# A sliding-window attention and GELU MLP stack on one core: a new written-out order of all engine queues

## The chip, the cores and the metric

The kernel runs on one NeuronCore of one Trainium2 chip. The metric is the time of one execution in device microseconds (us), less being better. A core has five engines that work through queues of their own, strictly in order, and that meet only at semaphores: PE (TensorE, matrix products), ACT (ScalarE, activation functions), DVE (VectorE), POOL (GpSimd) and SP (SyncE, which here only issues DMAs). PE writes its products into PSUM, which has eight banks of 512 float32 values per partition; ACT and DVE read them from there.

## What is computed

Two rounds of the same two layers over `x` of 2048 tokens by 512 channels in bf16. The attention has 32 heads of 16 channels and a causal window of 256 keys; the MLP is 512 to 1792 to 512 with a tanh GELU. The weights are the same in both rounds.

```python
def _A_ref(x, wqkv, wo):
    H = 32; Dh = D // H; W = 256
    q, k, v = (x @ wqkv) split into heads
    scores = einsum("bhqd,bhkd->bhqk", q, k) * (Dh ** -0.5)
    mask = (idx[:, None] - idx[None, :] >= 0) & (idx[:, None] - idx[None, :] < W)
    p = softmax(where(mask, scores, -1e9))
    o = einsum("bhqk,bhkd->bhqd", p, v)
    return o merged @ wo

def _B_ref(x, w1, b1, w2, b2):
    return gelu(x @ w1 + b1) @ w2 + b2

x = A_x
x = x + _A_ref(_layernorm(x), A_wqkv, A_wo)
x = x + _B_ref(_layernorm(x), B_w1, B_b1, B_w2, B_b2)
x = x + _A_ref(_layernorm(x), A_wqkv, A_wo)
x = x + _B_ref(_layernorm(x), B_w1, B_b1, B_w2, B_b2)
```

## The kernel before

**Tiles.** The 2048 tokens are 16 tiles of 128 rows, kept in SBUF as `X`. The two rounds make 32 tile passes, handled as 16 blocks of two tiles (block 0 to 7 are round one, 8 to 15 round two) for the attention, and as ten MLP jobs of two or four tiles (`JOBS`).

**The steps of a block.** For the layer norm DVE runs `bn_stats` (L588) and `bn_aggr` (L590), the inverse standard deviation is an add (`vp`, L594, POOL or DVE) and a power (`pw`, L600, POOL), and DVE writes the normalised tile `xn` (L610). A DMA transposes it (L615), except for the first four and the last two of the 64 normalised tiles, which PE transposes (`tp`, L622). Then PE makes Q and K (groups `q` and `k`, two each per block) and V (group `v`, one per tile); these, the output projection `op`, the first MLP product `m` (14 groups per job) and the second `y` (one per tile, 14 steps) are the *dense products*. All of them go through `pe_group` (L636): a group takes one PSUM bank at its first step, and its steps stand in the queue as nodes of their own (`m0_3.0`, `m0_3.1` and so on), so steps of other groups, or scores, can stand between them. The bank comes free when the group's result has been read out: K by DVE (`ke`, L670, 1.2 us), Q and V by DVE (L577) or ACT (L579), `op` and `y` by DVE (L832, L874), the first six `m` groups by DVE (L854) with a GELU on ACT afterwards (L857), the other eight by ACT (L862).

**Attention.** A block has ten *visits* (the first block of each round has five). A visit is one PE node `sc` (L737) that fills four banks with 2048 columns of scores, two ACT exponentials `ex` (L744), each of which reads two banks and frees them, and one to three masks `mk` (L765, DVE or POOL) that zero what lies outside the window in the exponentials. Twice per block a PE node `pv` (L787, 128 small matmuls, 64 in the first block of a round) multiplies the exponentials with V into two banks; DVE transposes those (`od`, L796), takes the reciprocal of the softmax sums (`rc`, L800), DVE or POOL normalises (`nm`, L804), and DVE transposes back (`ot`, L810) for the output projection.

**The order.** Nothing about the order is decided while the kernel is built. `_Plan.add` records 3080 nodes with their dependencies. Three written-out lists do the rest. `_ORDER` (L167) is one sequence of all nodes; each engine's queue is the nodes of that engine in that sequence. `_ALT` (L323) names the nodes that run on their other engine (masks and normalisations on POOL instead of DVE; Q and V read-outs and PE-transposed tiles on ACT instead of DVE; `vp` on DVE instead of POOL). `_BANKS` (L335) gives the PSUM bank of each allocation in turn:

```python
for i in _ALT:
    nodes[i]["eng"], nodes[i]["fn"] = nodes[i]["alts"][1]
banks = iter(_BANKS)
...
for i in _ORDER:
    nd = nodes[i]
    assert nd["deps"] <= seen
    for g, k in nd["alloc"]:
        b = next(banks)
        gmap[g] = tuple(range(b, b + k))
        free.difference_update(gmap[g])
    for g in nd["free"]:
        free.update(gmap[g])
```

`_Sched.op` (L62) then walks the sequence and gives each instruction the semaphore waits that its data and its banks require. A matmul that starts a group therefore waits for the read-out that last freed its bank.

Of the kernel before, what the change touches and what calls it, by code (L numbers as in the profile page):

```python
# [19 lines left out]
class _Sched:  # L20
# [147 lines left out]
    14, 33, 7, 4, 0, 29, 5, 34, 18, 3, 6, 13, 30, 37, 23, 39, 21, 1, 36, 8, 31, 22, 56, 35, 32, 16, 55, 15, 57, 58,  # L168
    60, 28, 46, 61, 59, 19, 41, 62, 2, 64, 20, 63, 40, 104, 65, 38, 24, 26, 9, 67, 66, 10, 52, 106, 68, 11, 27, 69,
    49, 107, 105, 80, 108, 81, 109, 82, 43, 83, 70, 12, 71, 110, 47, 72, 113, 73, 85, 84, 74, 111, 114, 86, 112, 87,  # L170
    115, 194, 152, 126, 195, 127, 128, 150, 116, 129, 196, 48, 117, 151, 153, 118, 130, 119, 154, 97, 120, 88, 197,
    98, 90, 89, 366, 99, 367, 155, 100, 91, 101, 75, 92, 368, 76, 158, 93, 102, 156, 198, 94, 77, 200, 369, 78, 131,
    79, 136, 96, 25, 132, 199, 137, 322, 159, 202, 138, 521, 203, 133, 201, 143, 139, 324, 95, 134, 144, 204, 135, 17,
    103, 121, 145, 140, 157, 216, 205, 146, 217, 122, 323, 123, 325, 147, 124, 326, 42, 327, 218, 125, 207, 45, 206,
    149, 212, 219, 208, 175, 214, 176, 142, 177, 178, 170, 213, 171, 179, 172, 370, 173, 372, 215, 160, 174, 161, 165,
    166, 371, 167, 168, 328, 374, 209, 162, 329, 375, 330, 163, 210, 519, 220, 376, 164, 331, 373, 221, 180, 169, 379,
    181, 148, 381, 377, 187, 211, 188, 189, 141, 182, 222, 380, 183, 223, 384, 190, 386, 224, 225, 382, 226, 50, 230,
    378, 231, 385, 232, 233, 227, 383, 228, 191, 342, 387, 388, 332, 333, 184, 234, 343, 192, 334, 229, 394, 185, 344,
    345, 237, 51, 335, 389, 336, 522, 235, 395, 236, 238, 346, 239, 396, 240, 243, 347, 520, 241, 244, 523, 398, 390,
    397, 337, 400, 338, 339, 639, 399, 352, 348, 242, 391, 349, 641, 340, 392, 350, 341, 402, 351, 359, 44, 404, 360,  # L180
    290, 361, 362, 353, 403, 363, 354, 524, 407, 640, 355, 408, 259, 306, 356, 252, 260, 245, 261, 253, 409, 357, 246,
    406, 254, 412, 358, 525, 255, 405, 413, 262, 247, 364, 256, 263, 257, 248, 414, 365, 249, 264, 563, 401, 193, 266,
    564, 411, 267, 415, 284, 186, 285, 416, 272, 565, 273, 269, 410, 275, 527, 270, 642, 250, 417, 528, 393, 566, 274,
    526, 287, 418, 288, 271, 427, 251, 428, 422, 423, 258, 53, 276, 419, 307, 265, 308, 420, 281, 309, 277, 310, 421,
    311, 54, 268, 312, 282, 286, 289, 278, 283, 424, 279, 425, 280, 313, 426, 529, 539, 540, 541, 432, 487, 567, 530,
    542, 568, 314, 643, 543, 315, 644, 531, 316, 569, 317, 318, 429, 645, 532, 647, 319, 646, 570, 433, 571, 533, 320,
    572, 430, 321, 291, 292, 648, 293, 573, 431, 576, 294, 896, 295, 578, 296, 575, 544, 434, 545, 297, 574, 546, 577,
    435, 581, 436, 547, 298, 583, 534, 548, 437, 649, 650, 535, 582, 651, 536, 898, 537, 652, 538, 299, 440, 549, 580,
    441, 591, 579, 550, 585, 592, 300, 551, 897, 653, 301, 552, 593, 302, 438, 595, 584, 303, 439, 304, 596, 899, 553,
    900, 586, 901, 305, 597, 554, 594, 599, 587, 555, 659, 598, 601, 660, 661, 662, 556, 600, 663, 557, 604, 558, 605,  # L190
    559, 602, 654, 560, 456, 457, 655, 606, 458, 561, 609, 603, 656, 445, 562, 610, 657, 608, 442, 443, 459, 607, 611,
    444, 446, 460, 463, 461, 452, 472, 447, 612, 478, 475, 658, 464, 664, 473, 902, 466, 465, 476, 469, 462, 613, 453,
    484, 903, 474, 454, 665, 479, 448, 588, 481, 485, 477, 467, 470, 486, 482, 589, 449, 480, 450, 468, 614, 451, 483,
    590, 471, 455, 666, 615, 683, 624, 625, 667, 616, 619, 488, 685, 904, 617, 489, 668, 490, 905, 491, 492, 684, 493,
    494, 503, 618, 495, 687, 626, 688, 686, 627, 620, 628, 496, 621, 689, 622, 631, 691, 497, 693, 498, 632, 690, 499,
    623, 500, 501, 692, 504, 502, 696, 505, 506, 697, 695, 694, 507, 629, 669, 670, 698, 630, 701, 1018, 671, 633,
    508, 1016, 703, 509, 700, 510, 511, 1017, 672, 634, 512, 702, 673, 711, 513, 699, 514, 713, 515, 705, 516, 517,
    704, 712, 715, 518, 1019, 637, 717, 706, 714, 638, 716, 719, 1020, 707, 1021, 721, 916, 917, 676, 718, 918, 720,
    1022, 724, 1024, 677, 919, 708, 725, 678, 722, 920, 679, 1023, 726, 729, 723, 680, 911, 730, 1025, 727, 906, 709,
    907, 908, 731, 940, 635, 675, 728, 912, 913, 942, 914, 732, 636, 933, 921, 733, 934, 909, 915, 710, 734, 941, 681,  # L200
    910, 682, 943, 944, 735, 935, 946, 674, 945, 736, 744, 936, 737, 922, 923, 937, 948, 947, 738, 924, 950, 745, 925,
    746, 848, 739, 747, 949, 740, 741, 748, 953, 742, 951, 955, 751, 926, 743, 954, 958, 952, 752, 927, 749, 928, 960,
    1036, 1037, 750, 956, 929, 1038, 753, 957, 959, 754, 930, 968, 1026, 757, 970, 1039, 755, 1027, 1028, 962, 756,
    969, 961, 972, 1029, 1040, 973, 758, 1030, 976, 931, 977, 963, 939, 978, 938, 786, 787, 788, 974, 979, 980, 775,
    776, 964, 777, 764, 789, 975, 965, 981, 790, 778, 971, 982, 781, 779, 765, 782, 983, 783, 784, 966, 986, 785, 766,
    988, 767, 984, 770, 768, 771, 772, 987, 773, 985, 1060, 774, 1061, 990, 1064, 989, 1065, 967, 991, 1066, 759, 992,
    1062, 760, 1067, 802, 797, 792, 798, 993, 1068, 832, 1275, 803, 1070, 761, 799, 793, 994, 762, 1069, 794, 763,
    1001, 812, 804, 1002, 1276, 995, 1071, 822, 795, 817, 1273, 800, 1003, 823, 769, 1274, 805, 1063, 1277, 824, 827,
    813, 1278, 806, 828, 825, 1004, 864, 1281, 801, 818, 807, 819, 826, 829, 996, 997, 780, 830, 1005, 1282, 833, 834,
    820, 1008, 791, 814, 998, 815, 1009, 835, 1072, 808, 816, 849, 836, 831, 837, 881, 850, 821, 838, 809, 810, 796,  # L210
    999, 851, 1000, 852, 811, 853, 854, 1279, 839, 1006, 1073, 1280, 855, 840, 1007, 841, 1393, 1031, 1075, 856, 857,
    1010, 1395, 1032, 842, 1074, 843, 858, 844, 1033, 1034, 1076, 1078, 1035, 845, 1080, 846, 1394, 859, 847, 1011,
    882, 883, 1079, 860, 1077, 884, 1014, 1088, 885, 1089, 1082, 1081, 861, 862, 1396, 886, 863, 887, 1090, 888, 1092,
    1041, 1094, 1042, 1043, 1397, 1044, 880, 1083, 1045, 1093, 1209, 1096, 1084, 889, 1097, 865, 1398, 866, 867, 890,
    1012, 1098, 868, 1091, 1101, 1013, 1085, 869, 1399, 1102, 870, 1100, 871, 1086, 872, 873, 891, 1103, 1106, 892,
    1095, 893, 1107, 1087, 874, 1104, 894, 875, 1105, 876, 1108, 1317, 1099, 877, 895, 878, 1319, 1283, 879, 1293,
    1294, 1284, 1109, 1318, 1295, 1321, 1110, 1296, 1323, 1285, 1320, 1297, 1286, 1111, 1322, 1225, 1287, 1325, 1112,
    1288, 1324, 1327, 1298, 1299, 1300, 1301, 1113, 1326, 1289, 1302, 1330, 1114, 1290, 1331, 1291, 1046, 1047, 1292,
    1328, 1048, 1121, 1332, 1115, 1049, 1335, 1050, 1122, 1337, 1123, 1333, 1124, 1116, 1051, 1125, 1117, 1336, 1118,
    1119, 1334, 1345, 1120, 1053, 1347, 1338, 1054, 1128, 1055, 1015, 1310, 1311, 1126, 1346, 1349, 1312, 1129, 932,  # L220
    1127, 1313, 1339, 1350, 1130, 1056, 1314, 1131, 1351, 1057, 1353, 1329, 1134, 1355, 1340, 1401, 1135, 1132, 1652,
    1354, 1358, 1348, 1133, 1341, 1360, 1303, 1357, 1304, 1305, 1352, 1306, 1359, 1307, 1363, 1052, 1364, 1361, 1437,
    1362, 1059, 1342, 1650, 1365, 1400, 1147, 1148, 1356, 1149, 1163, 1438, 1164, 1366, 1150, 1309, 1165, 1367, 1166,
    1439, 1308, 1653, 1651, 1368, 1167, 1654, 1343, 1402, 1151, 1441, 1440, 1369, 1136, 1443, 1158, 1159, 1137, 1241,
# [719 lines left out]
```

## Time and profile before

| | before |
|---|---|
| median of 3 runs | 446.42 us (446.25 to 447.74) |
| the profiled execution | 446.29 us |
| its span, first to last instruction | 444.6 us |
| PE busy | 426.6 us |
| ACT busy | 384.7 us |
| DVE busy | 346.5 us |
| POOL busy | 219.4 us |

The profiled execution lies 1.7 us above its own span and 0.13 us under the median. Matmuls are pipelined, so PE counts as busy also while the last product drains; its waits are read from the rows, not from the 96%.

### The profile page before, as it was taken

How to read it: one execution, taken by the hardware profiler on the slowest of the kernel's cores; microseconds unless marked ns; L12 is line 12 of the kernel's file. 1: busy time of each engine (PE TensorE's matmuls, PEld its weight loads, DVE VectorE, ACT ScalarE, POOL GpSimd, SP SyncE). 2: the span in 40 equal slices, each digit the busy share in tenths (PEclk: the TensorE clock that was granted, in tenths of full speed). 3: DMA queues.
4: the chain of work that ended last, by engine and by line, in shares of the span. 5: the costliest groups of instructions: out<-in, count | busy, mean ns of one | idle time of the engine just before them, and what ended most of it. 6: DMA issues, size and time to landing. Idle time of an engine off the chain costs nothing.

```text
span 444.6 us, 16910 instructions
## 1 busy us (share of the span) xinstructions
PE 426.6 (96%) x7579; PEld 230.9 (52%) x7579; DVE 346.5 (78%) x635; ACT 384.7 (87%) x452; POOL 219.4 (49%) x241
## 2 busy tenths in 40 slices
PE   7998999998789997999999999999999999999997
PEld 4555666644444563554455454464555464344673
DVE  7999988789876789985799886875898487746853
ACT  2997999999889899889899989999888988898642
POOL 5476255654352776732665336944726444604311
PEclk9999999999999999999999999999999999999999
DMA  8765432103201103310022021201341033001101
GB/s 227 217 156 146 100 106 50 27 15 65 43 4 23 12 7 62 66 33 13 3 59 43 16 47 14 42 13 27 63 56 45 1 51 89 25 1 38 39 0 49
DMA packets 47972, 23.25 MB, mean 52 GB/s; under 512 B 33180, under 2 KB 47900, under 8 KB 47900
## 3 DMA queue, kind: packets, MB, share of 16 engines
q1 hardware_dynamic: 47900, 22.17, 22.1%
q8 instruction: 60, 0.98, 1.0%
q14 instruction: 12, 0.10, 0.1%
HBM read 8.00 MB, written 2.10 MB: 23 GB/s over the span
## 4 chain that ended last, share of the span: by engine, by line
PE 84%; ACT 8%; DVE 5%; DMA 1%; issue 1%; SPq 1%
PE ps L636 65%; PE ps L737 9%; PE ps L787 9%; ACT E L744 8%; DMA b1raw<-in_B_b_dram 1%; DVE E L765 1%; DVE Va L577 1%; DVE stat L588 1%; DVE KT L670 1%; DVE OD L796 0%; SPq L542 0%; DVE X L874 0%; DVE xn L610 0%; SPq L537 0%; ACT QT L579 0%
## 5 line engine op out<-in xcount | busy, mean ns | idle before, releaser
L744 ACT ACTIVATE E<-ps 128x1024 bf16<-128x1024 f32 x300 | 284.1, 1032 | 30.4 <-PE ps L737 29.5
L765 POOL TENSOR_TENSOR E<-E,mask 128x512 bf16<-128x512 bf16 (+2 forms) x120 | 132.3, 1113 | 127.5 <-ACT E L744 127.1
L636 PE MATMUL ps<-W_sb,gT 128*128 128x512 bf16 x448 | 119.3, 380 | 0.0
L636 PE MATMUL ps<-xnTB,W_sb 128*128 128x512 bf16 (+1 forms) x560 | 116.9, 337 | 0.5 <-ACT E L744 0.5
L636 PE MATMUL ps<-xnTA,Wqkv_sb 128*128 128x256 bf16 x512 | 75.5, 273 | 2.1 <-ACT E L744 1.2
L636 PEld LDWEIGHTS ps<-xnTB,W_sb 128*128 128x128 bf16 x560 | 51.5, 98 | 42.2 <-issue 3.0
L737 PE MATMUL ps<-QT,KT 32*128 32x128 bf16 (+3 forms) x1920 | 60.1, 231 | 5.5 <-ACT E L744 4.2
L765 DVE TENSOR_TENSOR E<-E,mask 128x768 bf16<-128x768 bf16 (+2 forms) x116 | 53.7, 492 | 10.4 <-ACT E L744 10.2
L636 PEld LDWEIGHTS ps<-W_sb,gT 128*128 128x128 bf16 x448 | 39.9, 98 | 40.8 <-issue 3.0
L636 PEld LDWEIGHTS ps<-xnTA,Wqkv_sb 128*128 128x128 bf16 x512 | 47.0, 98 | 26.3 <-issue 3.3
L737 PEld LDWEIGHTS ps<-QT,KT 32*128 32x128 bf16 x1920 | 28.3, 92 | 55.7 <-ACT E L744 34.1
L796 DVE STREAM_TRANSPOSE OD<-ps 128x1024 f32<-128x1024 f32 x32 | 39.9, 1248 | 14.7 <-PE ps L787 14.3
L870 POOL TENSOR_TENSOR Xb<-X,b2all 128x512 f32<-128x512 bf16 x32 | 37.6, 1181 | 26.5 <-DVE X L832 14.1
L862 ACT ACTIVATE gT<-ps,b1T 128x512 bf16<-128x512 f32 (+1 forms) x80 | 43.3, 605 | 7.7 <-PE ps L636 7.6
L854 DVE TENSOR_SCALAR gT<-ps,b1T 128x512 bf16<-128x512 f32 (+1 forms) x60 | 37.0, 636 | 14.3 <-PE ps L636 13.7
L670 DVE TENSOR_TENSOR KT<-ps,parmask 128x1024 bf16<-128x1024 f32 x32 | 38.9, 1218 | 9.4 <-PE ps L636 9.0
L787 PE MATMUL ps<-E,Va 64*17 64x128 bf16 (+3 forms) x1920 | 43.9, 230 | 2.3 <-DVE E L765 1.0
L787 PE MATMUL ps<-E,Vs 64*17 64x128 bf16 (+3 forms) x1920 | 44.6, 230 | 0.4 <-issue 0.4
L787 PEld LDWEIGHTS ps<-E,Va 64*17 64x17 bf16 x1920 | 37.0, 84 | 12.4 <-issue 9.1
L588 DVE BATCH_NORM_STATS2 stat<-X 128x6 f32<-128x512 bf16 x64 | 42.7, 680 | 0.6
L636 PE MATMUL ps<-Wqkv_sb,xnTA 128*128 128x512 bf16 x128 | 39.2, 381 | 0.7 <-ACT E L744 0.4
L636 PE MATMUL ps<-Wo_sb,OT 128*128 128x512 bf16 x128 | 38.5, 380 | 0.8 <-DVE OD L796 0.7
(50 smaller groups left out, 348.5 us busy)
## 6 DMA issues: line engine op xcount, KB each, us to landing
Vs<-Va SPq DMA_DIRECT2D x64, 68.0 KB, 2.1
W_sb<-in_B_w_dram SPq DMA_DIRECT2D x4, 512.0 KB, 4.0
out_dram<-X SPq DMA_DIRECT2D x16, 128.0 KB, 1.9
X<-in_A_x_dram SPq DMA_DIRECT2D x3, 512.0 KB, 6.6
Wqkv_sb<-in_A_wqkv_dram SPq DMA_DIRECT2D x4, 256.0 KB, 5.1
W_sb<-in_B_w_dram SPq DMA_DIRECT2D x2, 384.0 KB, 5.7
W_sb<-in_B_w_dram SPq DMA_DIRECT2D x1, 768.0 KB, 8.7
Wqkv_sb<-in_A_wqkv_dram SPq DMA_DIRECT2D x1, 512.0 KB
```

What stands on the lines that cost most here:

```text
L577: return add("dve", lambda e, B: e.tensor_copy(dst(B), src(B)), reads=reads, writes=writes + ([] if free else reads), free=free, key=key, ...
L588: add("dve", lambda e, B, t=t, k6=k6: e.bn_stats(stat6[:, k6, :], X[:, t, :]), reads=["X%d" % t], writes=["st%d" % k6], key="bs%d" % (k + j))
L636: r = e.matmul(ps[:, B[g][0], cols], lhsT, rhs, start=st, stop=sp)
L670: add("dve", lambda e, B, g=g, i=i: e.tensor_tensor(out=KT[:, kb, 2 * i : 2 * i + 2].rearrange("p c m a q -> p a (c m) q"), in0=ps[:, B[g] ...
L737: x = e.matmul(ps[:, bk[r], o : o + n], KT[rows, kb, c, m].rearrange("p a q -> p (a q)"), QT[rows, c, q : q + n], start=True, stop=True)
L744: add("act", lambda e, B, g_=g_, gi=gi: e.activation(E[:, 2 * gi : 2 * gi + 2, e0 : e0 + 512], ps[:, B[g_][0] : B[g_][0] + 2, :], AF.Exp, ...
L765: fn = lambda e, B: e.tensor_tensor(out=Ew, in0=Ew, in1=Mw, op=ALU.mult)
L787: x = e.matmul(ps[32 * r : 32 * r + VW, B[g][par], c % 2 * 2 * P + lo : c % 2 * 2 * P + hi], V[rows, (2 * b + m // 2) % VR, c * HC + 2 * r ...
L796: add("dve", lambda e, B: e.transpose(OD[:, s].rearrange("p a c q -> p (a c q)"), ps[:, B[g][0] : B[g][0] + 2, :]), reads=["ps:" + g], wri ...
L854: add("dve", lambda e, B, g=g, fc=fc: e.tensor_scalar(out=gT[:, fc, c0 : c0 + M], in0=ps[:, B[g][0], 0:M], scalar1=b1T[:, fc : fc + 1], sc ...
L862: add("act", lambda e, B, g=g, fc=fc: e.activation(gT[:, fc, c0 : c0 + M], ps[:, B[g][0], 0:M], AF.Gelu_apprx_tanh, bias=b1T[:, fc : fc + ...
L870: add("pool", lambda e, B, t=t, xs=xs: e.tensor_tensor(out=Xb[:, xs, :], in0=X[:, t, :], in1=b2all[:], op=ALU.add), reads=["X%d" % t, "b2a ...
```

## The change

Only the three lists are replaced. No instruction is added or taken away and no shape changes; the functions are the same text. The diff is 360 lines of numbers; its core is this:

```diff
 _ORDER = [
-    14, 33, 7, 4, 0, 29, 5, 34, 18, 3, 6, 13, 30, 37, 23, 39, 21, 1, 36, 8, 31, 22, 56, 35, 32, 16, 55, 15, 57, 58,
...
-    3057, 3078, 3058, 3059, 3060, 3079, 3061, 3062,
...
+    3056, 3075, 3076, 3057, 3077, 3058, 3078, 3059, 3060, 3061, 3079, 3062,
 ]
...
 _ALT = [
-    62, 66, 74, 108, 112, 120, 140, 169, 184, 191, 197, 201, 210, 215, 219, 336, 341, 369, 373, 377, 382, 388, 392,
...
+    62, 66, 74, 112, 120, 140, 147, 169, 184, 197, 201, 206, 210, 215, 336, 341, 369, 373, 377, 378, 383, 388, 392,
...
 _BANKS = [
-    5, 6, 1, 6, 7, 2, 4, 1, 3, 2, 7, 2, 7, 4, 5, 0, 1, 4, 1, 0, 6, 7, 4, 5, 0, 2, 5, 4, 6, 3, 4, 0, 2, 6, 4, 0, 1, 3,
...
+    2, 4, 6, 0, 0, 6, 0, 6, 4, 6, 3, 6, 5, 4, 5, 6, 0, 5, 7, 6, 2, 3, 4, 0, 2, 3, 7, 2, 4, 2, 0, 5, 6, 0, 2, 3, 4, 6,
```

Put back into names, the lists say this. "Old" and "new" are counts of the lists themselves.

| read off the lists | old | new |
|---|---|---|
| nodes on their other engine (`_ALT`) | 175 | 171 (109 in both) |
| masks on POOL / on DVE | 120 / 116 | 108 / 128 |
| normalisations `nm` on POOL / on DVE | 19 / 13 | 23 / 9 |
| Q, V and transposed tiles read out by ACT | 24 | 27 |
| dense groups (of 300) whose steps stand side by side on PE | 35 | 64 |
| changes from one dense group to another in PE's queue | 898 | 783 |
| dense groups open at once, mean over PE's 1615 nodes | 2.31 | 1.98 |
| PE nodes at which five or more are open | 152 | 30 |
| runs of ACT of one kind (exponentials or GELUs) and their lengths | 18 | 18, the same lengths |

The beginnings of the queues, by node name:

```
PE  old: ... tp0 warm9 warm11 tp1 warm12 k0_0.0-.3 q0_0.0-.1 b1t q0_0.2-.3 k0_1.0 tp2 tp3 k0_1.1-.2 sc0_0
PE  new: ... tp0 tp1 warm1 k0_0.0-.3 q0_0.0-.1 tp2 q0_0.2-.3 k0_1.0 tp3 k0_1.1 b1t k0_1.2 sc0_0
SP  old: ldx0 ldx1 ldx2 ldw1_256 ldw1_0 ldw0_0 ldb2 ldb1 ldx4 ldw2_0 ldw0_256 ldz2 ldx8 ldu0 ...
SP  new: ldx0 ldx1 ldx2 ldw1_0 ldb1 ldw0_0 ldw1_256 ldx4 ldw2_0 ldw0_256 ldwo ldx8 ldu0 ...
ACT old: te0 qe0_0 te2 ex0_0_0 ex0_0_1 qe1_0 ... ex0_2_1 ve2 ex0_4_0 ex0_4_1
ACT new: te0 te2 qe0_0 ex0_0_1 ex0_0_0 qe1_0 ... ex0_2_1 ve2 ex0_4_1 ex0_4_0 ve3
POOL old: i7 i4 i0 i3 ia i1 j00 vp0 pw0 i2 pw1 j01 j10 i8 pw2 ...
POOL new: i7 i0 i4 i1 i3 i2 vp0 pw0 j00 pw1 ia vp2 pw2 j01 ...
```

Here `ldw1_0` loads the half of the K weights that `k0_0` reads, `ldw0_0` that of the Q weights for `q0_0`, `ldw1_256` the K weights for `k0_1`; `ldb1` loads the MLP bias that `b1t` transposes on PE (L561), `ldb2` the second bias, spread over all partitions (L570); `ia` is a memset of 1.2 us.

353 rows, old and new, of tables (_ALT, _BANKS, _ORDER) are left out of this document.

## The prediction

> **What bounds the kernel now.** I read the page's busy shares first, then the chain of work that ended last, the table by stages, the waits, and last the timeline of the start.
>
> ```profile
> span 444.6 us, 16910 instructions
> PE 426.6 (96%) x7579; PEld 230.9 (52%) x7579; DVE 346.5 (78%) x635; ACT 384.7 (87%) x452; POOL 219.4 (49%) x241
> ...
> PE 84%; ACT 8%; DVE 5%; DMA 1%; issue 1%; SPq 1%
> PE ps L636 65%; PE ps L737 9%; PE ps L787 9%; ACT E L744 8%; DMA b1raw<-in_B_b_dram 1%; DVE E L765 1%; DVE Va L577 1%; DVE stat L588 1%; DVE KT L670 1%; DVE OD L796 0%; SPq L542 0%; DVE X L874 0%; DVE xn L610 0%; SPq L537 0%; ACT QT L579 0%
> ```
>
> PE carries 84% of the chain, so time is won only where PE stands still, and lost wherever the new order makes it stand. ACT carries 8%, DVE 5%. The table by stages says where:
>
> ```profile
> 0.00:20.00 20.00, 17.40 (x156) 10.26 (x157) 16.85 (x35) 10.26 (x13) 9.81 (x25) 1.00 0.82 237
> 20.00:40.00 20.00, 17.84 (x430) 11.17 (x429) 19.38 (x36) 17.05 (x21) 12.69 (x14) 1.00 0.61 156
> ...
> 80.00:100.00 20.00, 19.23 (x431) 10.04 (x429) 15.42 (x32) 19.30 (x26) 10.88 (x13) 1.00 0.11 22
> 100.00:120.00 20.00, 16.32 (x431) 9.16 (x429) 17.25 (x32) 18.53 (x22) 7.70 (x8) 1.00 0.27 53
> 120.00:140.00 20.00, 18.46 (x269) 8.45 (x265) 15.03 (x26) 17.21 (x21) 11.54 (x12) 1.00 0.07 15
> ...
> 160.00:180.00 20.00, 17.64 (x540) 10.20 (x536) 18.61 (x36) 18.91 (x21) 13.82 (x15) 1.00 0.23 47
> ...
> 300.00:320.00 20.00, 20.00 (x449) 10.44 (x447) 13.62 (x23) 17.99 (x19) 11.26 (x11) 1.00 0.27 49
> ```
>
> Columns are the stretch, its length, PE, PEld, DVE, ACT and POOL busy, the granted clock (1.00, full), DMA share and GB/s. In the second half PE is full (20.00 of 20 at 300 to 320): the reorder can win nothing there except in the tail. PE's gaps lie in the first 20 us (2.6), at 20 to 40 (2.2), from 80 to 140 (0.8 + 3.7 + 1.5 = 6.0) and at 160 to 180 (2.4). In three of these stages, 80 to 120 and 160 to 180, ACT is busy 18.5 to 19.3 of 20, so most of what PE lacks there is ACT's own work, which the new order doesn't shorten. Who PE waits for:
>
> ```profile
> PEld ps L737 <- ACT E L744: 34.1, 77, 1.4
> ACT E L744 <- PE ps L737: 29.5, 48, 1.6
> ...
> PE ps L737 <- ACT E L744: 4.2, 7, 1.1
> PE ps L636 <- ACT E L744: 2.0, 3, 1.2
> ...
> PE ps L787 <- DVE E L765: 1.0, 2, 0.6
> ```
>
> The 34.1 us of the weight loads are mostly hidden behind products still in the array; where PE itself stood, the exponentials cost 4.2 + 2.0 = 6.2 us in all. That is the whole sum that freer banks could win back.
>
> **The change, term by term.** Work per engine barely moves. I counted the two order lists by name: dense steps between one score visit and the next are the same to within one or two steps nearly everywhere, and ACT's runs of exponentials and GELUs have the same lengths, so its table loads don't change. What differs is the start, the engines of some read-outs and masks, and how dense groups are interleaved.
>
> *The start.*
>
> ```profile
> 6.95 0.42 DVE L577 COPY xnTA<-ps 128x512 bf16<-128x512 bf16 x1 [0.17 <-PE ps L622]
> ...
> 7.29 0.24 DVE L590 BATCH_NORM_AGGREGATE statmv<-stat 128x2 f32<-128x6 f32 x2
> ...
> 7.81 1.47 PE L636 MATMUL ps<-xnTA,Wqkv_sb 128*128 128x256 bf16 x12 [0.27 <-DVE rstd L594]
> ...
> 8.55 0.81 DVE L610 TENSOR_SCALAR xn<-X,statmv,rstd 128x512 bf16<-128x512 bf16 x2 [0.82 <-POOL rstd L600]
> ...
> 9.87 0.18 PE L561 MATMUL ps<-ident,b1raw 14*128 14x14 bf16 x1 [0.59 <-DMA b1raw<-in_B_b_dram]
> ...
> 11.63 0.40 PE L737 MATMUL ps<-QT,KT 32*128 32x256 bf16 x8
> ```
>
> The bias transpose stands after 12 projection matmuls and holds PE 0.59 us for its DMA, which was issued eighth. In the new lists that DMA is fifth and the transpose stands six PE nodes later: the wait goes, -0.59. The first projection begins at 7.81 although its later input copy ended at 7.37 (6.95 + 0.42) and PE stood 0.27 before it; the DVE named is not its producer, so I take the wait to be for its weights, whose load was fifth and is now fourth, ahead of the load it stood behind: -0.27. What is late next is the transpose `tp2`, now ahead of the last two Q steps; it needs `xn2`, made at 8.55 so far. The 1.2 us memset `ia` now stands in POOL's queue before the add and power that `xn2` waits for, but these wait in any case for the statistics of tiles 2 and 3, the rows at 7.29, and the memset has the idle time before that, so I price it at nothing; if it starts later it costs up to its own 1.2. Sum -0.9, from +0.3 to -1.2 (a POOL that is late, a lighter DMA load without `ldb2`).
>
> *ACT.* Three more read-outs come to ACT in sum, one as early as the tenth exponential.
>
> ```profile
> L579 ACT ACTIVATE Va<-ps 128x512 bf16<-128x512 f32 x8 | 4.7, 616 | 0.0
> L765 POOL TENSOR_TENSOR E<-E,mask 128x512 bf16<-128x512 bf16 x71 | 82.7, 1169 | 68.3 <-ACT E L744 68.2
> L765 DVE TENSOR_TENSOR E<-E,mask 128x512 bf16<-128x512 bf16 x45 | 19.9, 446 | 4.0 <-ACT E L744 3.9
> L804 POOL TENSOR_TENSOR Nb<-OD,Rc 128x512 bf16<-128x512 f32 x19 | 20.2, 1063 | 20.7 <-DVE Rc L800 14.8 <-DVE rstd L594 5.6
> L804 DVE TENSOR_TENSOR Nb<-OD,Rc 128x512 bf16<-128x512 f32 x13 | 9.0, 689 | 0.3
> ```
>
> Each is 0.616 us. By the count ACT is one ahead up to the 110th exponential, two by the 130th; the third falls where PE is full and costs nothing. So 0.6 to 1.2 us where ACT sets the pace, 0 where it doesn't. I take +0.6, the lower end: of the whole chain only 8% is ACT's.
>
> *Masks and normalisations.* Twelve masks go from POOL to DVE (12 x 0.446 = +5.4 us of DVE at the middle shape) and four normalisations the other way (4 x 0.689 = -2.8); with three read-outs gone to ACT DVE's sum stays within 1 us. A mask's result comes 0.7 us sooner on DVE (1169 against 446); a normalisation 0.37 later on POOL, with other work to cover it. I price this at 0, from -1 to the rival below. The trace bears on contention too: DVE masks last 0.43 us at the median but 1.80 at the longest:
>
> ```profile
> L765 DVE TENSOR_TENSOR E<-E,mask x116: 259/426/1799, 21.2 to 415.5; 128x768 bf16<-128x768 bf16 x49, 128x512 bf16<-128x512 bf16 x45, 128x256 bf16<-128x256 bf16 x22
> ```
>
> The Trainium skill, "SBUF — State Buffer", section "Who interferes with whom", says that a DVE instruction with two SBUF inputs, which a mask is, and a GpSimd instruction that reads SBUF shut each other out for a whole instruction. The 1799 ns agree. By that rule twelve more masks become exposed to POOL on DVE, which is the mechanism of the second rival below.
>
> *Interleaving.* 64 dense groups of 300 now run in one piece (35 before), 2.0 are open on average (2.3), five or more at 30 PE nodes (152). A group's interleaving itself costs PE nothing:
>
> ```profile
> 339.56 10.25 PE ps L636 x48
> ```
>
> 48 steps of several groups took 10.25 us, 0.214 each. So the gain is only that read-outs come sooner and scores find banks. The bound is the 6.2 us that PE stood for exponentials; its other end is a loss of the same size, since blocks of one group can now stand before scores ACT is waiting for (its 29.5 us). In the lists scores take a bank freed at most two PE nodes before 80 times of 600 before, 73 of 599 after: a tenth fewer. So about a tenth to a fifth of 6.2 us; I take -1.2, the upper end, because the stretch with five open groups is the one that vanishes.
>
> *The tail.* The last tile's second product now ends three PE steps after its neighbour's, not four; its read-out queues at most 0.1 us. Left at 0.
>
> Sum: -0.9 + 0.6 + 0 - 1.2 = -1.5 us on the profiled execution's 446.29, which is 444.8 (that execution is 0.13 under the median). A difference of 0.3%, 1.3 us, is about what a measurement of this kernel can tell from no change: the forecast is just past it.
>
> **Rivals.** (1) *ACT takes it back.* If ACT sets the pace through 80 to 190 us, the start's 0.9 is met by 1.2 of extra read-outs, and freer banks meet no idle ACT. For it: ACT at 18.5 to 19.3 of 20; against: ACT itself waits 29.5 us for scores. Then 446.29 - 0.9 + 1.2 = 446.6, no change. (2) *Slower: PV waits for DVE masks.* In the new lists the last mask before a PV is on DVE for 26 of 32, and within two PE nodes of it for 14 (12 before). So far such a PV stood only twice, 0.5 us each. If the mask stands behind a normalisation (0.689) or is held by POOL, PE stands about 0.6 (the longest so far) for each. Against the forecast it decides from five of the fourteen on (3.0 us); at seven it is 4.2, and the time 449.0. For it: DVE is busy 19.4 of 20 at 20 to 40 us and 18.6 at 160 to 180; against: a mask is sooner on DVE. (3) *The gaps close.* Half of the 2.2 + 6.0 + 2.4 us of PE's gaps goes too: 444.8 - 5.3 + 1.2 = 440.7.
>
> **How the numbers follow.** The forecast has 0.34, the closing gaps 0.08, ACT's return 0.24, late PVs 0.34: a list of 3080 places rearranged has many places where PE can come to stand in a half of the run where it now never does, and each costs in full. So faster by over 0.3% 0.42, within 0.24, slower 0.34. The range leaves out the two far ends: from 441.5, short of the third rival, to 449.5, a little past the second; the forecast's own runs from 443.0 to 445.0.
>
> **What would show it.** Right: the wait for b1raw is gone and the first score begins at about 10.7 instead of 11.63; PE's gaps from 80 to 140 fall from 6.0 to under 5; PE stays at 20.0 of 20 from 240 to 420. Wrong: `PE ps L787 <- DVE E L765` grows from 1.0 to 3 or more; ACT's busy time is up by 1.8 and the chain's ACT share by half a per cent with it; or stages after 240 us show a PE under 19.5. What would unmake the forecast is any single new stall of 2 us in the second half.

## The result and the profile after

The changed kernel takes 444.86 us at the median (22 runs, 443.48 to 448.35), the kernel before 446.95 in the same comparison (22 runs, 446.25 to 449.32). The ratio is 0.9955, with a 95% interval of 0.994 to 0.9971: faster by 0.45%, or 2.0 us. The profiled execution took 444.66 us, its span is 442.8, 1.8 less than the span before.

The head of the page after, its chain by engine, and some lines of its waits in which PE stands for somebody (us in total, times, longest):

```profile
span 442.8 us, 16903 instructions
...
PE 424.7 (96%) x7579; PEld 230.2 (52%) x7579; DVE 343.9 (78%) x641; ACT 385.3 (87%) x455; POOL 210.4 (48%) x232
...
PE 84%; DVE 8%; ACT 5%; issue 1%; POOL 1%; DMA 0%; DVEq 0%
```
```profile
PE ps L737 <- ACT E L744: 3.6, 11, 0.7
...
PE ps L636 <- ACT E L744: 1.4, 3, 0.8
...
PE ps L737 <- DVE gT L854: 1.1, 3, 0.6
PE ps L737 <- DVE QT L577: 0.9, 1, 0.9
PE ps L737 <- DVE Va L577: 0.9, 1, 0.9
PE ps L787 <- DVE E L765: 0.9, 2, 0.5
```

PE stood 6.2 us for exponentials before and stands 3.6 + 1.4 = 5.0 now. But it stands more for DVE: over all lines of that view 7.8 us against 5.6, two of the new ones being scores before a Q or a V read-out, 0.9 each. Span less busy time is 444.6 - 426.6 = 18.0 before and 442.8 - 424.7 = 18.1 after. So the gain is not found in PE's idle time as a sum, and has to be found by place. The stages (columns as in the prediction):

```profile
80.00:100.00 20.00, 18.96 (x433) 10.24 (x432) 16.97 (x36) 19.41 (x26) 6.70 (x9) 1.00 0.13 30
100.00:120.00 20.00, 16.52 (x434) 9.43 (x433) 18.00 (x35) 19.05 (x23) 9.05 (x9) 1.00 0.35 64
120.00:140.00 20.00, 18.91 (x268) 9.11 (x268) 13.46 (x27) 18.08 (x23) 7.89 (x8) 1.00 0.01 2
...
300.00:320.00 20.00, 20.00 (x443) 10.29 (x442) 15.06 (x28) 18.61 (x21) 10.01 (x11) 1.00 0.27 50
```

A better ruler than fixed stretches of time are milestones that both kernels pass with nearly the same work done (between two of them the number of dense products differs by 3 at most, that of the much shorter score products by 12): the 32 DVE transposes that follow the 32 PVs (L796). Three of them in the timeline of DVE, before, and then after (start, duration):

```profile
106.52 1.25 DVE L796 STREAM_TRANSPOSE OD<-ps 128x1024 f32<-128x1024 f32 x1 [0.57 <-PE ps L787]
...
129.58 1.25 DVE L796 STREAM_TRANSPOSE OD<-ps 128x1024 f32<-128x1024 f32 x1 [1.60 <-PE ps L787]
...
417.86 1.24 DVE L796 STREAM_TRANSPOSE OD<-ps 128x1024 f32<-128x1024 f32 x1
```
```profile
107.02 1.25 DVE L796 STREAM_TRANSPOSE OD<-ps 128x1024 f32<-128x1024 f32 x1 [0.39 <-PE ps L787]
...
128.60 1.25 DVE L796 STREAM_TRANSPOSE OD<-ps 128x1024 f32<-128x1024 f32 x1 [0.96 <-PE ps L787]
...
416.06 1.25 DVE L796 STREAM_TRANSPOSE OD<-ps 128x1024 f32<-128x1024 f32 x1
```

These are the 8th, the 10th and the last. With the same reading of every kernel of this study, the time from one milestone to another is:

| us | to 1st | 1st to 8th | 8th to 10th | 10th to 18th | 18th to last | last to end |
|---|---|---|---|---|---|---|
| before | 23.43 | 83.09 | 23.06 | 94.34 | 193.94 | 26.71 |
| after | 22.81 | 84.21 | 21.58 | 94.63 | 192.83 | 26.79 |
| difference | -0.62 | +1.12 | -1.48 | +0.29 | -1.11 | +0.08 |

So the change loses 1.1 us on the way to 107 us, wins 1.5 in the 23 us after that, and wins about 1.1 after 224 us, in the part where PE counts as full (20.00 of 20) in both kernels. Two of these numbers need care. The time to the 1st milestone varies from one execution to another: in the eight profiles of this study whose lists begin as the old one does, it lies between 22.63 and 24.20. And part of the 1.1 after 224 us is work that was moved, as the account of the prediction shows.

### The profile page after: what moved, and what is told of

The parts are those of the page before. It is cut to its first block, busy times and chain, and to the rows that moved or that the text cites. A ratio compares the mean times of both kernels' runs of the same rounds, so it can differ in the third digit from the quotient of the medians.

```text
span 442.8 us, 16903 instructions
## 1 busy us (share of the span) xinstructions
PE 424.7 (96%) x7579; PEld 230.2 (52%) x7579; DVE 343.9 (78%) x641; ACT 385.3 (87%) x455; POOL 210.4 (48%) x232
## 4 chain that ended last, share of the span: by engine, by line
PE 84%; DVE 8%; ACT 5%; issue 1%; POOL 1%; DMA 0%; DVEq 0%
PE ps L636 65%; PE ps L737 10%; PE ps L787 9%; ACT E L744 5%; DVE KT L670 1%; DVE E L765 1%; DVE gT L854 1%; DVE stat L588 1%; DVE xn L610 1%; DVE OD L796 1%; DVE X L832 1%; DVE Va L577 1%; DMA X<-in_A_x_dram 0%; POOL rstd L600 0%; DVE OT L810 0%
## 5 line engine op out<-in xcount | busy, mean ns | idle before, releaser
L765 POOL TENSOR_TENSOR E<-E,mask 128x512 bf16<-128x512 bf16 (+2 forms) x108 | 118.7, 1114 | 96.2 <-ACT E L744 95.9
L636 PE MATMUL ps<-W_sb,gT 128*128 128x512 bf16 x448 | 118.1, 380 | 0.0
L636 PE MATMUL ps<-xnTB,W_sb 128*128 128x512 bf16 (+1 forms) x560 | 113.8, 337 | 0.0
L636 PE MATMUL ps<-xnTA,Wqkv_sb 128*128 128x256 bf16 x512 | 74.1, 273 | 1.3 <-ACT E L744 0.6
L765 DVE TENSOR_TENSOR E<-E,mask 128x512 bf16<-128x512 bf16 (+2 forms) x128 | 61.6, 504 | 10.5 <-ACT E L744 10.0
L796 DVE STREAM_TRANSPOSE OD<-ps 128x1024 f32<-128x1024 f32 x32 | 39.9, 1248 | 25.3 <-PE ps L787 24.1
L804 POOL TENSOR_TENSOR Nb<-OD,Rc 128x512 bf16<-128x512 f32 x23 | 24.4, 1062 | 38.8 <-DVE Rc L800 36.6
```

What stands on the lines that cost most here:

```text
L636: r = e.matmul(ps[:, B[g][0], cols], lhsT, rhs, start=st, stop=sp)
L765: fn = lambda e, B: e.tensor_tensor(out=Ew, in0=Ew, in1=Mw, op=ALU.mult)
L796: add("dve", lambda e, B: e.transpose(OD[:, s].rearrange("p a c q -> p (a c q)"), ps[:, B[g][0] : B[g][0] + 2, :]), reads=["ps:" + g], wri ...
L804: return e.tensor_tensor(out=Nb[:, s, :].rearrange("p (k a d) -> p a k d", a=2, d=Dh), in0=sums[:, :, :, 0:Dh], in1=rc[:, :, :, None].to_b ...
```

## The experiments

The kernels below have their lists wrapped in fewer lines, so their line numbers are 15 lower: L722 are the scores, L729 the exponentials, L750 the masks, L595 the normalised tiles. "Old" and "new" are the lists before and after. In a spliced list each node brings its engine and, where that bank is free, its bank from the list that it comes from. Place 780 of the order is passed at about 107 us, 900 at about 128, 1524 at about 218. Three explanations stood against each other first: the list of engines does it; the start does it; the order of one or a few places does it.

### Is it the engines or the order?

e1_alt_only is the kernel before with the new `_ALT` alone:

```diff
 _ALT = [
-    62, 66, 74, 108, 112, 120, 140, 169, 184, 191, 197, ...
+    62, 66, 74, 112, 120, 140, 147, 169, 184, 197, 201, ...
```

> Old order and old banks, only the list of alternate engines is the new one. Place theory (the gain is made by the new order of the stretch from 107 to 128 us, and some more after 240 us): no gain, ratio to the kernel before 1.000, between 0.997 and 1.003. Engine theory (twelve masks less on POOL make masks come sooner, and that is the gain): the whole gain, ratio 0.9955 and POOL about 9 us less busy.

e2_order_only is the reverse, the new `_ORDER` and `_BANKS` with the old `_ALT`.

> New order and new banks with the old list of alternate engines. Place theory: most of the gain stays, ratio 0.994 to 0.998. Engine theory: the gain is gone, ratio 1.000 or above.

Measured: e1 463.25 us, ratio 1.0356 [1.0321, 1.0391]; e2 458.43 us, ratio 1.0251 [1.0223, 1.0279]. Either half alone makes the kernel slower, by 3.6 and 2.5%. Both expectations of the place theory missed. Of the engine theory's, e2 has the ratio above 1.000, but e1, which was to have the whole gain, refutes the theory. The page of e1 (busy, and chain by engine) and its groups by shape:

```profile
PE 429.6 (93%) x7579; PEld 230.6 (50%) x7579; DVE 359.6 (78%) x641; ACT 387.2 (84%) x455; POOL 211.3 (46%) x232
...
PE 62%; DVE 19%; ACT 9%; DMA 3%; POOL 3%; issue 2%; SPq 1%; DVEq 0%
```
```profile
L750 DVE TENSOR_TENSOR E<-E,mask 128x768 bf16<-128x768 bf16 x49 | 34.3, 723 | 6.1 <-ACT E L729 6.0
L595 DVE TENSOR_SCALAR xn<-X,statmv,rstd 128x512 bf16<-128x512 bf16 x64 | 33.4, 539 | 6.3 <-POOL rstd L585 5.4 <-DMA xnTA<-xn 0.5 <-DMA xnTB<-xn 0.2
```

The same two groups after, with the same engine list:

```profile
L765 DVE TENSOR_TENSOR E<-E,mask 128x768 bf16<-128x768 bf16 x49 | 30.2, 634 | 4.6 <-ACT E L744 4.2
...
L610 DVE TENSOR_SCALAR xn<-X,statmv,rstd 128x512 bf16<-128x512 bf16 x64 | 27.6, 447 | 5.3 <-POOL rstd L600 5.3
```

The instructions are the same and as many, yet a mask of 768 columns lasts 723 ns against 634 and a normalised tile 539 against 447 (598 and 480 before). DVE is busy 359.6 us against 343.9, and it carries 19% of the chain instead of 8%. e2 has the same mark: DVE 359.1 us, 20% of the chain. What differs is the work beside them. By the starts and ends in the traces, a DVE instruction that overlaps none on POOL lasts the same in all four kernels: the mask of 768 columns 549 to 551 ns at the median, the normalised tile 404 to 406. Those that overlap one are longer: 953 ns on average for 21 of these masks in e1, 805 for 16 after. Summed over all shapes with five or more instructions, what the overlapping instructions last beyond the undisturbed ones is 24.0 us in e1 and 26.7 in e2, and 9.8 both before and after. That is 14 of the 16 us that DVE is busier in e1 than after. The Trainium skill, "SBUF — State Buffer", section "Who interferes with whom", says that DVE in a two-port mode and GpSimd exclude each other for a whole instruction, whoever comes first, which bears on the normalised tiles. Its rule for masks stands in the prediction. Two experiments below, at the start and at 115 us, show single collisions of that kind. So the order and the engine list were made for each other in what they let run side by side: an engine list is good or bad only with its order.

### Where in the run is it?

Four splices, cut at 107 and 128 us:

```diff
+e4_new_first107: _ORDER = new[:780] + rest of old
+e5_new_107_128:  _ORDER = old[:780] + new[:900] not yet placed + rest of old
+e6_old_first128: _ORDER = old[:900] + rest of new
+e7_old_first107: _ORDER = old[:780] + rest of new
```

> The first 780 places of the new lists (to about 107 us, the start included), then the rest of the old ones, each node on the engine that its own lists give. Place theory: the second projection output comes out 0.4 to 0.5 us later than before, as it did in the whole change, and nothing makes up for it: ratio 1.001. Start theory (the gain is begun by the earlier first score, 11.31 against 11.63, and by the state of the queues that follows from it): ratio 0.997 or lower.

> Old lists, with only the places 780 to 900 (about 107 to 128 us) in the new order, on the new engines and banks. Place theory: the 1.0 to 1.5 us that the whole change wins there are won here too, ratio 0.9965 to 0.998, and the tenth transposed PV comes 1 us sooner. If the win needs what came before it: ratio 1.000.

> The first 900 places of the old lists (to about 128 us), then the rest of the new ones. Place theory: the 1.0 to 1.5 us won at 107 to 128 us are missing, the 0.7 us won after 240 us are there: ratio 0.998 to 0.999. Rival (everything after the first hundred us only carries on what was won there): ratio 1.000.

> The first 780 places of the old lists (to about 107 us, with the old start), then the rest of the new ones. Place theory: the whole gain without the 0.4 us that the new lists lose up to there: ratio 0.994 to 0.996, no slower than the changed kernel. Start theory: the gain is gone, ratio 0.999 or above.

Then two with a cut at 218 us:

```diff
+e9_new_second_half: _ORDER = old[:1524] + rest of new
+e10_new_107_218:    _ORDER = old[:780] + new[:1524] not yet placed + rest of old
```

> The first 1524 places of the old lists (to about 218 us, where both lists have run the same set of nodes, so the joint is clean), then the rest of the new ones. Place theory: the later 0.7 us by themselves, ratio 0.998 to 0.999, transposed PVs of the second half coming gradually earlier, the last by 0.6 to 0.9 us. Rival (the later gain is only carried from 107 to 133 us): 1.000.

> Old lists, with the places 780 to 1524 (about 107 to 218 us) from the new ones, both joints clean or nearly so. Place theory: the gain of that stretch with all of its end, 1.2 to 1.5 us against the old start, ratio 0.9965 to 0.9975, and hardly any execution with a drop of the granted clock. Rival (what is won comes after 218 us): 0.999 to 1.000.

Measured, with the milestones of the profiled executions (a ratio is against the kernel before on the same chip, whose medians lay between 446.62 and 447.67 in these comparisons; it is not the quotient of two medians, but within 0.002 of it):

| | us | ratio | 1st to 8th | 8th to 10th | 10th to 18th | 18th to last |
|---|---|---|---|---|---|---|
| before | 446.95 | | 83.09 | 23.06 | 94.34 | 193.94 |
| after | 444.86 | 0.9955 [0.994, 0.9971] | 84.21 | 21.58 | 94.63 | 192.83 |
| e4, new to 107 | 447.97 | 1.0013 [0.9992, 1.0033] | 84.51 | 23.01 | 94.42 | 193.96 |
| e5, new 107 to 128 | 446.40 | 0.9976 [0.9959, 0.9992] | 83.13 | 22.32 | 94.33 | 194.22 |
| e6, new from 128 | 448.08 | 1.0003 [0.9984, 1.0023] | 83.10 | 24.65 | 96.09 | 192.82 |
| e7, new from 107 | 445.42 | 0.9948 [0.9931, 0.9964] | 83.14 | 22.16 | 95.50 | 192.84 |
| e9, new from 218 | 446.38 | 0.9988 [0.9973, 1.0003] | 83.14 | 23.40 | 95.14 | 192.95 |
| e10, new 107 to 218 | 445.86 | 0.9969 [0.9952, 0.9987] | 83.18 | 21.78 | 95.29 | 193.97 |

The columns mostly add up like building blocks. Whoever has the old list up to 107 us takes 83.1 to the 8th milestone; the two with the new one 84.2 and 84.5. From the 8th to the 10th it is 23.0 with the old list (e9's 23.40 has the old list there too) and 21.6 to 22.3 with the new. From the 18th on it is 193.9 to 194.2 old (one profile below, e8's, has 194.84), and 192.8 to 193.0 in all six kernels with the new list there (after, e6, e7, e9, and e3 and e12 below). The exception is the 10th to the 18th. In e9 and e10 the excess lies in the one interval that holds the joint at 218 us (16th to 17th milestone: 5.00 and 5.09 us, against 3.98 to 4.10 in the others). In e7 it lies between the 14th and the 15th (12.96 us, 12.08 in e12 with the same list there) and stays unexplained. e6's 96.09 holds most of a drop of its clock (last section).

The start theory falls: e4 wins nothing and e7 wins everything without the new start. The place theory holds for 107 to 128 us, where e5 and e10 are faster with intervals clear of 1, and e4, e5, e7 and e10 have the ratios that it forecast. But a part of these ratios is the granted clock, of which the last section tells. Of the 75 executions of the kernel before in these comparisons, 18 show a mean clock of 0.996 or less and take about 2 us longer; of the 30 of e5, e7 and e10 none does, as was expected for e10, but none of e9's 12 either, which has the old list at this place. Among executions without the mark the median of e5 is 0.5 us under that of before, that of e10 0.7 and that of e7 1.9. e9's own interval reaches 1.0003, so that the second half alone pays is shown by the milestones of six profiles and not by its time: what it wins after the 18th milestone, 1.0 us, is about what its joint costs just ahead of it. e6's time tells nothing, and missed what was expected: its joint at 128 us costs more than the place before it could bring (8th to 10th 24.65).

What the place at 107 to 130 us looks like, in the timelines of ACT before and after:

```profile
109.31 8.56 ACT L744 ACTIVATE E<-ps 128x1024 bf16<-128x1024 f32 x9
...
118.38 2.85 ACT L744 ACTIVATE E<-ps 128x1024 bf16<-128x1024 f32 x3 [0.51 <-PE ps L737]
...
122.53 7.44 ACT L744 ACTIVATE E<-ps 128x1024 bf16<-128x1024 f32 x8 [1.29 <-PE ps L737]
...
131.43 1.94 ACT L744 ACTIVATE E<-ps 128x1024 bf16<-128x1024 f32 x2 [1.47 <-PE ps L737]
```
```profile
111.74 9.27 ACT L744 ACTIVATE E<-ps 128x1024 bf16<-128x1024 f32 x10 [0.19 <-PE ps L737]
...
122.00 7.58 ACT L744 ACTIVATE E<-ps 128x1024 bf16<-128x1024 f32 x8 [0.99 <-PE ps L737]
...
130.36 1.94 ACT L744 ACTIVATE E<-ps 128x1024 bf16<-128x1024 f32 x2 [0.78 <-PE ps L737]
```

Before, ACT stands 0.51 + 1.29 + 1.47 = 3.27 us for scores between its long runs; after, 0.19 + 0.99 + 0.78 = 1.96. The third of these waits lies behind the 10th milestone. The two stretches from the 8th milestone to the 10th count only what lies between them:

```profile
106.52:129.58 23.06, 18.56 (x449) 9.46 (x444) 19.07 (x33) 20.80 (x23) 10.91 (x12) 1.00 0.14 31
```
```profile
107.02:128.60 21.58, 18.04 (x446) 9.37 (x443) 19.11 (x36) 20.20 (x23) 9.96 (x9) 1.00 0.23 40
```

ACT is idle 23.06 - 20.80 = 2.26 us before and 21.58 - 20.20 = 1.38 after, so 0.9 of the 1.48 us. PE is idle 4.50 us before and 3.54 after; the other 0.5 is busy time with nearly as many products.

### Which move makes it? Two tries that failed

Before, the last score visit of the long run waits 1.11 us for an exponential to free its banks:

```profile
117.92 0.40 PE L737 MATMUL ps<-QT,KT 32*128 32x192 bf16 x12 [1.11 <-ACT E L744]
```

e8_bank_swap gives it other banks: the old lists, with banks 0, 1 and 4, 5 exchanged from that visit (`sc4_7`) on. e11_three_moves does that, and also moves the two masks `mk4_4_1` and `mk4_4_0` behind the Q read-out `qe7_0`, the second of them to POOL. In the new lists, too, neither is on DVE ahead of that read-out:

```diff
 e8, e11: from sc4_7 on
-banks 0, 1, 4, 5
+banks 4, 5, 0, 1
 e11:
-... mk4_4_1 mk4_4_0 ... qe7_0 ...        mk4_4_0 on DVE
+... qe7_0 mk4_4_1 mk4_4_0 ...            mk4_4_0 on POOL
```

> Old order and old engines; from the eighth visit of block 4 on the bank labels 0, 1 and 4, 5 are exchanged, so that this visit's second half takes the banks that K and Q read-outs freed, instead of those of the exponential just ahead of it, and the PV behind it takes the latter. Nothing else changes. Bank theory (between 107 and 121 us ACT stood because a score had to wait for the exponential just before it): ACT's wait of 0.51 us at 118.4 goes, the tenth transposed PV comes 0.4 to 0.8 us sooner, ratio 0.998 to 0.999. Rival (the stretch is won by masks and read-outs moved to other engines): no difference at that place, ratio 1.000.

> Old lists with three small moves around the eighth visit of block 4, all taken from the new lists: the two masks that stand ahead of the Q read-out on DVE go behind it, one of them to POOL, and the banks are exchanged as in the bank swap. Theory (order, engine and bank have to fit: the swap alone failed because the bank it gave the score came free from a Q read-out that stood behind masks): the score at 117.9 no longer waits for the exponential, PE's wait there falls from 1.1 to 0.5 us or less and the ninth transposed PV comes 0.4 to 0.9 us sooner, ratio 0.998 to 0.999. Rival (only the whole stretch does it): no gain at that place, 1.000 or above.

Measured: e8 448.09 us, ratio 1.0000 [0.9981, 1.0018]; e11 448.35, ratio 1.0024 [1.0009, 1.0040]. Both are slower just there, 24.65 and 24.87 us from the 8th to the 10th milestone against 23.06. The timeline of PE in e8:

```profile
118.69 0.40 PE L722 MATMUL ps<-QT,KT 32*128 32x192 bf16 x12 [1.63 <-DVE QT L562]
```

The wait for the exponential is gone; a later one for a Q read-out on DVE stands in its place, and the visit begins at 118.69 instead of 117.92. e11 shows why moving a mask to POOL does not mend that:

```profile
115.03 2.09 DVE L595 TENSOR_SCALAR xn<-X,statmv,rstd 128x512 bf16<-128x512 bf16 x2
...
115.33 1.64 POOL L750 TENSOR_TENSOR E<-E,mask 128x768 bf16<-128x768 bf16 x1 [0.34 <-ACT E L729]
...
118.99 0.51 PE L722 MATMUL ps<-QT,KT 32*128 32x192 bf16 x12 [2.05 <-DVE QT L562]
```

The mask on POOL runs beside two normalised tiles, which last 2.09 us; in e8, without it, they last 0.73 (115.14, x2). Read-outs behind them on DVE are late by that, and the score waits 2.05. The changed kernel has the same mask on POOL beside the same two tiles:

```profile
115.16 0.74 DVE L610 TENSOR_SCALAR xn<-X,statmv,rstd 128x512 bf16<-128x512 bf16 x2 [0.21 <-POOL rstd L600]
115.59 1.79 POOL L765 TENSOR_TENSOR E<-E,mask 128x768 bf16<-128x768 bf16 x1 [0.47 <-ACT E L744]
```

There the second tile starts at 115.48, 0.11 us ahead of the mask, and lasts 0.41; in e11 it starts at 115.35, 0.02 us behind the mask, and lasts 1.76. So a tenth of a microsecond decides whether this move costs 1.4 us, and e11 doesn't take over what decides it: in the new lists `mk4_4_0` stands ahead of `qe7_0`, and a third mask, `mk4_3_1`, has also gone behind that read-out. Neither a bank nor these three moves make the gain; which of the nodes rearranged between 107 and 128 us do is open. One difference was not tried by itself: in the new list the two exponentials of a visit stand side by side on ACT, in the old one some stand apart.

### Why the start won less than predicted, and what it could win

e3_ia_early is the changed kernel with one node of POOL's queue, the memset `ia`, back ahead of `i1`:

```diff
 POOL
-i7 i0 i4 i1 i3 i2 vp0 pw0 j00 pw1 ia vp2 pw2 ...
+i7 i0 i4 ia i1 i3 i2 vp0 pw0 j00 pw1 vp2 pw2 ...
```

> The changed kernel with one node moved: the memset of the ones column of V, which lies in POOL's queue behind the second power and runs at 5.61 to 6.78 us, goes back ahead of the identity's first cut. Port theory (the DVE normalisation at 5.75 lasts 1.18 instead of 0.40 because POOL's memset holds it up): that normalisation lasts 0.40 again, the first projection starts 0.4 to 0.7 us sooner than 8.15 and the first score at about 10.8; of that 0 to 0.7 us reach the end, ratio 0.993 to 0.9955. Rival (the late first projection comes from its weights): the normalisation is short, the projection still starts near 8.15.

The start after, and that of e3, from the timelines:

```profile
5.61 1.17 POOL L525 MEMSET Va<- 128x256 bf16 x1
...
5.75 1.18 DVE L610 TENSOR_SCALAR xn<-X,statmv,rstd 128x512 bf16<-128x512 bf16 x1
...
8.15 1.47 PE L636 MATMUL ps<-xnTA,Wqkv_sb 128*128 128x256 bf16 x12 [0.55 <-issue]
...
10.88 0.18 PE L561 MATMUL ps<-ident,b1raw 14*128 14x14 bf16 x1
...
11.31 0.40 PE L737 MATMUL ps<-QT,KT 32*128 32x256 bf16 x8
```
```profile
5.76 0.40 DVE L595 TENSOR_SCALAR xn<-X,statmv,rstd 128x512 bf16<-128x512 bf16 x1
...
7.38 1.47 PE L621 MATMUL ps<-xnTA,Wqkv_sb 128*128 128x256 bf16 x12 [0.56 <-ACT xnTA L564]
...
10.54 0.40 PE L722 MATMUL ps<-QT,KT 32*128 32x256 bf16 x8
```

Measured: 444.30 us, ratio 0.9929 [0.9902, 0.9956], span 442.0. With the memset on POOL beside it, the second normalised tile lasts 1.18 us; without, 0.40. Those 0.78 us go on to the first projection (8.15 against 7.38) and to the first score (11.31 against 10.54), and the milestones of e3 keep 0.8 to 0.9 of it to the last (415.22 against 416.06). The intervals of e3 and of the changed kernel overlap, so the gain over it rests on the profiles. That it is the memset, and not one execution, fourteen profiles show: this tile lasts 1.18 or 1.19 us in the three with the late memset (after, e2, e4), and 0.40 in the eleven others.

They also show how much the start varies. In the eight whose lists begin as the old one does, the transpose of b1raw waits 0 to 1.27 us for its DMA and the first score comes at 10.64 to 12.39. In the five that begin in the new order the transpose never waits, and the first score comes at 11.31 to 11.53 with the late memset and at 10.54 and 10.88 (e3, e12) with the early one.

e12_join tries for a version that beats both: the start of e3, the old list from its 100th place to 107 us, where the new one loses 1.1, and the new list from there.

```diff
+e12_join: _ORDER = e3[:100] + old[:780] not yet placed + rest of e3
```

> A version made of the parts that won: the first 100 places of the new lists with the memset moved back as in the run with the early memset (the start), the old lists up to place 780, the new ones from there on. If the parts add up: 0.9 us of the start and 1.8 us of the rest, ratio 0.992 to 0.994. If the old lists waste the early start by 107 us: 0.995, as with the old start.

Measured: 444.32 us, ratio 0.9931 [0.9909, 0.9953]. The stretch from the 1st milestone to the 8th is back at 83.17 us, but the 1st comes at 23.77 instead of 22.03. Of these 1.7 us, 0.3 are there at the first score, where the two lists are still the same; the other 1.4 come behind the joint at place 100, and take back what the old list wins. It is no better than e3.

## Why the prediction was right or wrong

**The time.** 444.8 was forecast and 444.86 measured; the profiled execution fell by 446.29 - 444.66 = 1.6 where the sum said 1.5. The terms did not come out as well as their sum, and that the sum fits is in part luck: a loss of 1.1 us before 107 us and a gain after 224, neither of which it contains, about cancel.

**The start, -0.9: mis-sized.** The mechanism held: the transpose of b1raw waits for nothing (before: 0.59). The -0.27 for the weights of the first projection is not seen: before's 7.81 is the latest of the eight profiles with the old start (7.33 is the earliest), and in e3 the projection, at 7.38, stands 0.56 for its input copy. The first score came at 11.31, not at 10.7, and the gain there is 0.32. The step that failed is the memset `ia` "priced at nothing": I looked for its cost in POOL's queue, where there was none, and not on the engine beside it. It cost 0.78 through DVE, and with it moved (e3) the first score comes at 10.54, a gain of 1.09, and in e12 at 10.88. By the first milestone the changed kernel has 0.62, less than two executions with the same start can differ by there (22.63 to 24.20).

**ACT, +0.6: not seen.** ACT's busy time grew by 0.6 us, not by the 1.85 of three read-outs, and its share of the chain fell from 8 to 5%. No profile shows this cost; it may be part of the 1.1 us that the new list loses before 107 us. That loss is in no term of the sum, and no run took it apart.

**Masks and normalisations, 0: right as a sum, wrong in kind.** Both signs that it named stayed: PV waits for DVE masks 0.9 us (1.0 before), and DVE's sum fell by 2.6. But the engine list by itself costs 3.6% (e1) and the order without it 2.5% (e2). The time that DVE lost beside POOL is 9.8 us before and after, and 24 to 27 in those two. A term that is the small rest of two large ones can't be priced by counting instructions.

**Interleaving, -1.2: right in size, and partly in place.** PE's waits for exponentials fell by just 1.2, from 6.2 to 5.0, but its waits for DVE grew from 5.6 to 7.8, and its idle time didn't fall, so that the size fits is luck. What was won is 1.48 us between 107 and 130 us, where ACT's idle time falls by 0.9, and 1.11 after 224. The sign given for it failed: PE's gaps from 80 to 140 fell to 1.04 + 3.48 + 1.09 = 5.6, not under 5.

**"In the second half the reorder can win nothing": wrong.** PE stays at 20.00 of 20 from 240 to 420, as predicted, and yet this part became shorter. Two stretches from the 18th milestone to the last, before and after:

```profile
223.92:417.86 193.94, 193.92 (x3438) 99.12 (x3437) 148.31 (x267) 178.90 (x203) 95.56 (x101) 1.00 0.19 38
```
```profile
223.23:416.06 192.83, 192.81 (x3435) 98.94 (x3434) 147.91 (x272) 178.16 (x203) 92.33 (x93) 1.00 0.17 36
```

Busy time itself fell by 1.11 us. Three dense products fewer lie in it, about 0.64 at the 0.214 of the prediction's row. These are not won but moved: two are done before the 18th milestone instead (x1694 against x1692 from the 10th to the 18th) and one after the last (x158 against x157). From the 10th milestone to the last it is 288.28 us before and 287.46 after, 0.8 less with one product fewer, so about 0.6 is won. Of the 1.11, some 0.5 is left in which as many products as before are done in less busy time, so the column counts stalls as busy; that they are the draining of the last product is argued and not shown. That a full PE leaves nothing to win was read out of a column that can't show it. What made these stalls shorter was not isolated.

**Tail, 0: right.** From the last milestone to the end it is 26.71 us before and 26.79 after, with one product more.

**Rivals.** ACT's return (446.6) and the late PVs (449.0) are refuted by the chain's 5% and the 0.9 us above. The gaps did not close (440.7): 5.6 of 6.0 remain at 80 to 140, and PE's busy time at 20 to 60 is 18.65 + 17.68 against 17.84 + 18.98, so the gaps there grew by 0.5.

## What to carry to other kernels

Compare two orders of the same work by milestones, not by stretches of time or by an engine's idle sum: the time between two instructions that both kernels contain shows at once where an order wins and where it loses, and mostly adds up over splices. Count the products between two milestones too, since work that was moved across one looks like time won. Before an instruction is moved to or along POOL's queue, look at what DVE does in that microsecond: a 1.2 us memset that delays nothing on its own queue cost 0.8 us through its neighbour, and a mask that starts 0.02 us ahead of a tile cost 1.4 where one 0.11 us behind it cost nothing. And a searched order and its choice of engines come as one piece: either without the other was 2.5 to 3.6% slower, and single moves taken from it won nothing, while whole stretches of it, order and engines together, could be grafted.

## What the hardware showed that was not expected

**POOL holds up DVE even when it only writes.** The memset reads nothing, and a DVE tensor_scalar of 0.40 us beside it took 1.18. The Trainium skill, "SBUF — State Buffer", section "Who interferes with whom", lets a tensor_scalar in a two-port mode be blocked for the whole instruction by any GpSimd instruction that came first, and the row agrees: memset from 5.61 to 6.78, tensor_scalar from 5.75 to 6.93. The prediction used that section only for masks.

**The clock fell after a thin stretch of PE.** In e8, stretches of 1.5 us around the late score visit (columns as in the stages above; the granted clock stands behind POOL):

```profile
115.00:116.50 1.50, 1.21 (x16) 0.82 (x16) 1.48 (x5) 1.50 (x3) 0.10 (x1) 1.00 0.00 0
116.50:118.00 1.50, 0.56 (x10) 0.11 (x2) 1.50 (x3) 1.50 (x2) 0.00 (x0) 1.00 0.43 87
118.00:119.50 1.50, 0.81 (x60) 0.71 (x61) 0.54 (x1) 0.48 (x2) 0.00 (x0) 1.00 0.43 87
119.50:121.00 1.50, 1.43 (x96) 1.18 (x89) 0.00 (x0) 1.50 (x3) 0.00 (x0) 0.55 0.44 101
121.00:122.50 1.50, 1.23 (x3) 0.46 (x3) 1.39 (x2) 0.99 (x2) 1.34 (x2) 0.50 0.23 49
122.50:124.00 1.50, 1.50 (x17) 0.59 (x15) 0.68 (x3) 0.00 (x0) 1.50 (x2) 0.81 0.00 0
```

PE is busy 0.56 and 0.81 of 1.5 us, and then runs about 3.4 us at half clock. In the same 3 us PE is busy 0.61 + 1.12 before and 0.39 + 1.27 after, and the clock stays at 1.00: there a little more than half of the time did not bring it down. e11 has such a drop at 119.2 us, e2 at 122.3, e1 one of twice the length at 124.4, and e6 one at 130.0, across the 10th milestone. So part of what e8 and e11 lose from the 8th to the 10th milestone is this clock, and not the order as such: 3.4 us at half clock cost up to 1.7, an estimate. Not every execution of a kernel has it; the mark of a mean clock of 0.996 or less is in 7 of e8's 12 and in 9 of 12 of e6 and of e11 each. Among executions without it e8's median is level with that of before (447.25 against 447.28) and e11's, of three, is 1.2 above, so the two tries win nothing either way. The Trainium skill, "TensorE: Matmul & The Clock Gate", section "What's actually happening", has PE at half clock after at least one idle window of about 3.4 us, and at full clock after at least one busy one. Length and depth agree with the rows above; but here PE was not idle in the time before, only thin.
